# Moving one projection row tile into the attention loop, with early normalisation of half of x and spread stack transfers

## The chip, the core and the metric

The kernel runs on one core of a Trainium2 chip. The metric is the device time of one execution in microseconds (us); three runs of the kernel before gave 1792.6, 1792.7 and 1793.6.

## What is computed

x is 2048 x 640 (S x D). Branch A is self-attention with 32 heads of 20 columns, branch B a two-layer network over the token axis (F = 1728), and a sigmoid gate per token mixes them:

```python
    g = _sigmoid((x * gate_w).sum(-1, keepdims=True))
    a = _A_ref(x, A_wqkv, A_wo)      # softmax(q k^T / sqrt(20)) v, then @ wo
    b = _B_ref(x, B_w1, B_b1, B_w2, B_b2)
    # _B_ref: h = layernorm(x); u = gelu(h^T w1 + b1); y = (u w2 + b2)^T
    return g * a + (1 - g) * b
```

Everything is float32. Products that need it are made of a high and a low float32r part in three passes (high x high, high x low, low x high).

## The kernel before

The kernel is one long stream for TensorE (PE), whose order is written out by hand; ScalarE (ACT), VectorE (DVE), GpSimd (POOL) and SyncE (SP, which issues most transfers) also run in the order in which the code names their instructions. A queue that waits holds up all that is named after it on that queue. Five stages follow each other:

**Projections of q, k and v.** Units of one 128 x 512 output tile (`qk_unit`), 15 matmuls each. ACT copies the high part out of PSUM (`evh`, 3 buffers), DVE subtracts the low part (`evl`, 2 buffers), SP stores both in DRAM. The PSUM tiles go round four banks (`one_tile`). The last 24 units (the loop over `units`, line 545) also prepare the first half of the layer norm for branch B: `h_load` (SP) brings 128 x 320 of x, `h_norm` normalises it on POOL, `h_split` makes the high part on ACT and the low one on POOL. In each unit these stand ahead of the unit's own copies.

**Branch B** (`mlp`). The width D is done in two halves d = 0, 1; each has 14 row tiles of u and 16 of y, in matmuls over 64 rows that go in pairs (`pair64`). Between them the planner (line 796) puts steps of the s stream, which computes raw scores to find the softmax's maxima: `s_one`, `s_over` and `s_two` each use a PSUM bank that DVE's reduction must empty. `dve_room` says how many s steps may have been made at which point. For d = 1 the halves of x are loaded and normalised during d = 0's y tiles, by DVE (`h_norm(1, t)`, line 753). The operand stacks of the next head pair come by many small transfers that are queued in `drip` and issued by SP one per two s steps, among the loads of branch B's weights (`w_raw`, line 512), which ACT and POOL must split before PE uses them. The last stack, for the first attention pair, comes this way too, with the maxima (`load_m`) and `load_v(0)` behind it.

**The attention loop** (line 1005). 16 head pairs x 32 iterations. An iteration issues the score matmuls `st_pair` and `st_one` twice, two s steps while any are left (`take`), and the pv matmuls of the iteration before (`pv_flush`). ACT's three exponentials empty the score banks; the bank pair `two` is there once. The s steps run out in the last pair's iteration 7. After every 16 iterations `pv_evac` copies the result, stores it in `o_d` and the row sums in `l_d`, and `norm_steps` later makes reciprocals and broadcasts them to `r_d`. For the last four heads that chain runs behind the loop (`last_norm`).

**Output projection** (`a_tile`, line 1085). Sixteen row tiles t of 128 rows. Heads 0 to 25 fill four 128-row chunks (`e_load`, `e_high`, `e_low`: load o and the reciprocals, multiply, split), the last heads the fifth (`l_load`, `l_high`, `l_low`). Tiles 0 to 7 use the first four chunks (24 matmuls); from t = 8 each tile uses all five (30), with the missing fifth of tile t - 8 behind it (6). Each tile takes two banks from `st_tile`, which alternates the bank pair `two` and the banks `one0`, `one1`; DVE empties them (line 1072) into `tys`.

## Time and profile before

| | us |
|---|---|
| median of three runs | 1792.7 |
| profiled execution | 1796.8 |
| its span, first to last instruction | 1794.7 |
| PE busy | 1779.3 |
| ACT busy | 1481.1 |
| DVE busy | 1236.7 |
| POOL busy | 640.7 |

The span is one profiled execution; the device time of the same execution is 2.1 us longer, and the median of the runs without a profile is 4.1 us below it. A busy PE counts matmuls from issue to modelled end, so that its share says little where PE waits for less than a matmul's length. TensorE's granted clock is at its full level, 2.4 GHz, in every slice of the page.

### The profile page before, as it was taken

To read this page: it belongs to the slowest core of one execution; us is meant where nothing else is said; L and a number is where in the kernel's file an instruction comes from. 1 tells how busy PE (TensorE), PEld (TensorE's weight loads), DVE (VectorE), ACT (ScalarE), POOL (GpSimd) and SP (SyncE) were. 2 spreads that over 40 slices of the span, in tenths; PEclk is the share of its full clock that TensorE was granted. 3 is DMA by queue.
4 is the path that set the end of the run, shared out by engine and by line. 5 is a ranking of instruction groups with operands and counts; after the bars stand their busy time and mean duration, and the time that the engine had idled before them with its cause. 6 is when DMAs were issued, how large, how long until landed. Compare 5 with 4: busy or idle time off the path is not lost.

```text
span 1794.7 us, 39876 instructions
## 1 busy us (share of the span) xinstructions
PE 1779.3 (99%) x14976; PEld 1113.8 (62%) x14976; DVE 1236.7 (69%) x2394; ACT 1481.1 (83%) x2534; POOL 640.7 (36%) x898
## 2 busy tenths in 40 slices
PE   9999999999999999999999999999999999999998
PEld 7998899999999999633333333333333333333388
DVE  5303289999889999777767677676777777767244
ACT  4244388887878886699999999999999999999930
POOL 1123377778877767211111111121332121212210
PEclk9999999999999999999999999999999999999999
DMA  8757876647675564325213223052363232301653
GB/s 292 241 173 245 258 188 170 161 152 193 175 180 161 144 183 142 90 57 131 59 30 82 61 68 83 18 105 70 46 138 69 52 86 59 73 13 25 216 154 125
DMA packets 157937, 222.95 MB, mean 124 GB/s; under 512 B 68590, under 2 KB 95614, under 8 KB 154318
## 3 DMA queue, kind: packets, MB, share of 16 engines
q1 hardware_dynamic: 139568, 190.74, 39.0%
q0 software_dynamic: 15440, 24.45, 5.8%
q10 hardware_dynamic: 2736, 5.21, 1.0%
q8 instruction: 118, 1.93, 0.5%
q14 instruction: 75, 0.61, 0.1%
HBM read 165.43 MB, written 54.54 MB: 123 GB/s over the span
## 4 chain that ended last, share of the span: by engine, by line
PE 93%; DVE 3%; DMA 3%; ACT 0%; issue 0%; SPq 0%; POOL 0%; ACTq 0%; DVEq 0%; POOLq 0%
PE pv L899 29%; PE st L986 20%; PE s L208 12%; PE u L48 10%; PE y L48 8%; PE qk L54 6%; PE v L54 4%; PE a L1066 3%; DVE mx L214 1%; DMA xr<-in_xT_dram 1%; DVE ov L233 1%; DVE oy L1072 1%; DVE xm L481 1%; DMA wr<-in_w_dram 0%; DMA rbl<-r_d 0%
## 5 line engine op out<-in xcount | busy, mean ns | idle before, releaser
L214 DVE TENSOR_REDUCE mx<-s 128x1 f32<-128x512 f32 x1280 | 834.4, 686 | 282.0 <-PE s L208 216.8
L1001 ACT ACTIVATE p<-st 128x512 f32<-128x512 f32 x1022 | 583.1, 657 | 1.1 <-PE st L986 1.1
L993 ACT ACTIVATE p<-st 128x1024 f32<-128x1024 f32 x511 | 552.4, 1081 | 2.8 <-PE st L986 2.2
L899 PE MATMUL pv<-p,v 128*32 128x512 f32 x4088 | 547.2, 605 | 0.0
L986 PEld LDWEIGHTS st<-qs_True,ks_True 62*128 62x128 f32 x2044 | 245.8, 184 | 432.1 <-ACT p L993 427.0
L986 PE MATMUL st<-qs_True,ks_True 62*128 62x512 f32 x2044 | 495.2, 446 | 0.0
L208 PE MATMUL s<-ks_False,qs_False 60*128 60x512 f32 x1152 | 340.1, 396 | 4.8 <-DVE mx L233 1.9
L43 POOL TENSOR_TENSOR wl<-wr,wh 128x512 fp32r<-128x512 f32 x228 | 275.5, 1219 | 80.3 <-ACT wh L40 64.8
L233 DVE CUSTOM_DVE_ANT_0 ov<-s,ov 128x512 f32<-128x512 f32 x384 | 263.6, 687 | 38.9 <-PE s L208 28.7
L223 ACT ACTIVATE ov<-s 128x512 f32<-128x512 f32 x384 | 226.4, 597 | 68.4 <-PE s L208 62.7
L208 PE MATMUL s<-sk,sq 60*128 60x512 f32 x896 | 279.7, 394 | 0.0
L879 POOL DMA_DIRECT2D l_d<-oev x128 | 62.7, 496 | 459.1 <-DVE oev L872 459.0
L48 PE MATMUL y<-gh,wh 64*128 64x320 f32 x896 | 223.1, 307 | 0.0
L48 PE MATMUL y<-gl,wh 64*128 64x320 f32 x832 | 214.7, 306 | 0.0
L48 PE MATMUL y<-gh,wl 64*128 64x320 f32 x832 | 214.1, 305 | 0.0
L208 PEld LDWEIGHTS s<-ks_False,qs_False 60*128 60x128 f32 x1152 | 190.0, 185 | 11.6 <-DVE mx L233 4.9
L899 PEld LDWEIGHTS pv<-p,v 128*32 128x32 f32 x4088 | 82.6, 108 | 174.9 <-issue 162.4
L40 ACT ACTIVATE wh<-wr 128x512 fp32r<-128x512 f32 (+3 forms) x247 | 147.0, 599 | 43.1 <-PE y L48 15.7
L48 PE MATMUL u<-hh,wh 64*128 64x320 f32 x864 | 178.7, 307 | 0.0
L48 PE MATMUL u<-hl,wh 64*128 64x320 f32 x864 | 178.6, 307 | 0.0
L208 PEld LDWEIGHTS s<-sk,sq 60*128 60x128 f32 x896 | 166.0, 185 | 18.1
L48 PE MATMUL u<-hh,wl 64*128 64x320 f32 x800 | 167.8, 307 | 0.0
(137 smaller groups left out, 2339.3 us busy)
## 6 DMA issues: line engine op xcount, KB each, us to landing
wr<-in_w_dram SPq DMA_DIRECT2D x192, 256.0 KB
ks_True<-k_d SPq DMA_DIRECT2D x96, 160.0 KB
qs_True<-q_d SPq DMA_DIRECT2D x192, 80.0 KB
qs_False<-q_d SPq DMA_DIRECT2D x108, 80.0 KB
sk<-k_d SPq DMA_DIRECT2D x42, 160.0 KB
sq<-q_d SPq DMA_DIRECT2D x84, 80.0 KB
v_d<-vt SPq DMA_DIRECT2D x32, 168.0 KB
v<-v_d SPq DMA_DIRECT2D x16, 336.0 KB
```

Of the source, the lines that this page charges most:

```text
L40: nc.scalar.activation(hi, src, AF.Copy)
L43: (lo_eng or nc.vector).tensor_sub(lo, src, hi.bitcast(F32))
L48: nc.tensor.matmul(ps[k], a[r], b[r], start=start, stop=stop)
L54: nc.tensor.matmul(ps, a, b, start=(i == 0 and k == 0), stop=(i == n - 1 and k == 2))
L208: nc.tensor.matmul(ps, qs[half][r, t * P:(t + 1) * P], ks[r, kc * 512:(kc + 1) * 512], start=True, stop=True)
L214: nc.vector.tensor_reduce(mx[:, slot, j, t: t + 1], ps, axis=AX.X, op=OP.max)
L223: nc.scalar.activation(over[j, kc], ps, AF.Relu)
L233: nc.vector.tensor_tensor_reduce(ov, ps, ov, 1.0, -3.0e38, OP.add, OP.max, mx[:, slot, j, t: t + 1])
L899: nc.tensor.matmul(pv[r: r + 32, :], v_tiles[p][:, kt, 10 * j: 10 * j + 32], pt[j, c], start=(kt == 0), stop=(kt == NT - 1))
L986: nc.tensor.matmul(ps, ks[r, kt * P:(kt + 1) * P], qs[qh][r, c * 512:(c + 1) * 512], start=True, stop=True)
L993: nc.scalar.activation(pt, ps, AF.Exp, scale=SCALE)
L1001: nc.scalar.activation(pt, ps, AF.Exp, scale=SCALE)
```

## The change

Four edits.

- **A projection tile in the loop.** Row tile 0's first four chunks are multiplied inside the last head pair: 24 `pair64` in two halves of 320 columns (`row_half`, `first_row`), one or two per iteration from 10 to 31, in the two `s` banks. `e_load(0)` moves to iteration 0, `e_high(0)` and `e_low(0)` to 5, the second ones to 24. The first iteration of the loop takes no s steps.
- **The last reciprocals.** The last `l_d` stores, their load, the store of the reciprocals (now 4 x 2048 in `rc_d`) and four loads that broadcast them go through SP; o's last chunk is one load. `l_high` goes behind the tile's evacuation.
- **Early normalisation.** In the 24 units x's second half is loaded (`n_load`), normalised by DVE and stored in `xn_d` (`n_store`), both transfers from POOL, in 3 buffers; branch B's second half then loads it ready, and `h_norm(1, t)` goes, with its part of `dve_room`.
- **Spread transfers.** `drip` is issued every fourth s step (every second one before step 128), the first attention stack in the gaps between (`slow`), `load_v(0)` in 8 pieces.

```diff
+    rc_d = dram.tile([LAST, S], F32, name="rc_d")
+    xn_d = dram.tile([S, HALF], F32, name="xn_d")
...
-        nc.sync.dma_start(xm, x[t * P:(t + 1) * P, d * HALF:(d + 1) * HALF])
+        rows = slice(t * P, (t + 1) * P)
+        nc.sync.dma_start(xm, xn_d[rows] if d else x[rows, :HALF])
...
+    def n_load(t):
+        xns[t] = hp.tile([P, HALF], F32, tag="ty", bufs=3, name=f"xn1_{t}")
+        nc.gpsimd.dma_start(xns[t], x[t * P:(t + 1) * P, HALF:])
+
+    def n_store(t):
+        xn = xns.pop(t)
+        nc.vector.tensor_scalar(xn, xn, negm[:, t:t + 1], rstd[:, t:t + 1], op0=OP.add, op1=OP.mult)
+        nc.gpsimd.dma_start(xn_d[t * P:(t + 1) * P], xn)
...
         if 2 <= n < NT + 2:
-            h_norm(0, n - 2)
+            h_norm(n - 2)
+        if 4 <= n < NT + 4:
+            n_store(n - 4)
+        if 2 <= n < NT + 2:
+            n_load(n - 2)
...
-                        h_norm(1, 0)
-                    if t + 1 < NT:
-                        later_on(2500, lambda t=t: h_norm(1, t + 1))
...
     def dve_room(n):
-        norms = min(max((n - U_STEPS) / (NT * 40), 0), 1) * NT * NORM
-        return (dve_work(S_AHEAD) + NT * NORM) * (n + 1 - FIRST) / (STEPS - 20 - FIRST) - norms
+        return dve_work(S_AHEAD) * (n + 1 - FIRST) / (STEPS - 20 - FIRST)
...
             if done == 4 * 128 + 40:
+                held, drip[:] = list(drip), []
                 st_src[0] = base_stack(0, True, None)
...
-                drip.append(lambda: load_v(0))
-            if drip:
+                load_v(0, 8, put)
+                slow[:], drip[:] = drip, held
+            if drip and (done % 4 == 0 or done < 128):
                 drip.pop(0)()
+            elif slow and done % 4 == 2:
+                slow.pop(0)()
...
+    def last_load():
+        b = LAST * S // P
+        rl = ap.tile([P, 256], F32, tag="rl", bufs=1, name="rl_last")
+        nc.sync.dma_start(rl[:, :b], l_d[H - LAST:].rearrange("h (a b) -> (h a) b", b=b))
+        last_rl.append(rl[:, :b])
+
+    def last_recip():
+        nc.vector.reciprocal(last_rl[0], last_rl[0])
+        nc.sync.dma_start(rc_d.rearrange("h (a b) -> (h a) b", b=LAST * S // P), last_rl[0])
...
-                nc.gpsimd.dma_start(l_d[h: h + 1, cols], ev[r + DH: r + DH + 1, :])
+                put = nc.sync if (p, qh) == (NP - 1, 1) else nc.gpsimd
+                put.dma_start(l_d[h: h + 1, cols], ev[r + DH: r + DH + 1, :])
...
+    def l_load():
+        raw, rb = [ap.tile([P, 4, 512], F32, name=f"{n}l") for n in ("or", "rb")]
+        r0 = (NC - 1) * P
+        nc.gpsimd.dma_start(raw.rearrange("p a b -> p (a b)"), o_d[r0:])
+        rb = rb.rearrange("p a b -> p (a b)")
+        nc.gpsimd.dma_start(rb[:L0], r_v[r0:r0 + L0])
...
+    def l_rest(rb):
+        for h in range(LAST):
+            nc.sync.dma_start(rb[L0 + h * DH:L0 + (h + 1) * DH], rc_d[h:h + 1].broadcast_to([DH, S]))
...
+    def row_half(c):
+        row_ps[:] = [s_tile([P, HALF], f"a0_{c}_{k}") for k in range(2)]
+        oh, ol = o_hl[0]
+        cols = slice(c * HALF, (c + 1) * HALF)
+        passes = [e for k in range(NC - 1) for e in ((oh[:, k, :P], woh[k]), (oh[:, k, :P], wol[k]), (ol[:, k, :P], woh[k]))]
+        for i, (a, b) in enumerate(passes):
+            row_mms.append((list(row_ps), a, b[:, cols], i == 0, i == len(passes) - 1))
+
+        def evac(ps=list(row_ps)):
+            for k in range(2):
+                nc.vector.scalar_tensor_tensor(tys[0][:, cols], ps[k], g_t[:, :1], tys[0][:, cols], op0=OP.mult, op1=OP.add)
+
+        row_evacs.append(evac)
+
+    def first_row(it):
+        if it in (10, 21):
+            row_half(it // 21)
+        for _ in range(2 if it in (14, 18, 26) else 1):
+            if row_mms:
+                pair64(*row_mms.pop(0))
+        if it == 19:
+            row_evacs.pop(0)()
...
-                if it in (16, 20, 26, 30):
-                    e_load((16, 20, 26, 30).index(it))
+                if it in (0, 16, 26, 30):
+                    e_load((0, 16, 26, 30).index(it))
...
-                if it in (20, 26):
-                    e_high(it // 26, ap, nc.gpsimd)
-                    e_low(it // 26, nc.gpsimd)
+                if it in (5, 24):
+                    e_high(it // 24, ap, nc.gpsimd)
+                    e_low(it // 24, nc.gpsimd)
...
-            take = min(LEFT - given, 2)
+            take = min(LEFT - given, 2) if p or it else 0
             g = p * 32 + it
             if g:
                 st_pair(g)
+                if p == NP - 1:
+                    first_row(it)
                 st_one(g, 0)
...
     pv_flush()
+    assert not row_mms
+    row_evacs.pop(0)()
...
-        for n in lates:
-            l_high(n)
-        evacs = [(t, range(NC) if t >= NT // 2 else range(NC - 1))]
+        evacs = [(t, range(NC) if t >= NT // 2 else range(NC - 1))] if t else []
...
+        for n in lates:
+            l_high(n)
...
-        if t == 1:
-            last_norm[1][0]()
-            for f in last_norm[2]:
-                f(nc.sync.dma_start)
-            for n in (2, 0, 3, 1):
-                nc.gpsimd.dma_start(*late_args[n][1])
+        if t == 2:
+            last_recip()
+            l_rest(last_rb)
```

## Rows read from the trace of the kernel before

**Rows 1.** The page: busy time, share of the span, instructions

```profile
PE 1779.3 (99%) x14976; PEld 1113.8 (62%) x14976; DVE 1236.7 (69%) x2394; ACT 1481.1 (83%) x2534; POOL 640.7 (36%) x898
```

**Rows 2.** Windows: length, busy PE PEld DVE ACT POOL, clock, DMA share, GB/s

```profile
136.00:220.00 84.00, 84.00 (x362) 67.77 (x361) 24.69 (x38) 31.50 (x58) 28.84 (x35) 1.00 0.80 248
600.00:700.00 100.00, 100.00 (x1235) 99.75 (x1234) 90.71 (x229) 82.90 (x162) 72.51 (x76) 1.00 0.56 161
1668.00:1712.00 44.00, 44.00 (x282) 15.73 (x285) 4.03 (x4) 44.00 (x71) 12.91 (x16) 1.00 0.65 220
```

**Rows 3.** Waits of PE, whole span: us in total, times, longest us

```profile
PE a L1066 <- DVE oy L1072: 3.5, 8, 1.7
PE s L208 <- DVE mx L233: 1.9, 9, 0.3
PE s L208 <- DVE mx L214: 1.3, 1, 1.3
PE s L208 <- ACT ov L223: 1.3, 2, 1.0
```

**Rows 4.** Chain that ended last, branch B: start us, us, what

```profile
393.52 1.02 DVE xm L481
...
459.79 1.02 DVE xm L481
...
521.68 4.72 DMA wr<-in_w_dram
```

**Rows 5.** Timeline of SP's queue, 500 to 528: start us, us, instructions

```profile
514.68 2.08 SPq L808 DMA_DIRECT2D qs_True<-m_d  x3
```

**Rows 6.** Timeline, all engines, first two iterations of the loop

```profile
740.01 0.61 DVE L692 TENSOR_SCALAR ty<-y,omg,b2o 128x320 f32<-128x320 f32 x1 [3.79 <-PE s L208]
...
741.94 1.09 PE L208 MATMUL s<-ks_False,qs_False 60*128 60x512 f32 x2 [1.33 <-DVE mx L214]
...
742.97 1.07 PE L899 MATMUL pv<-pf,v 128*32 128x512 f32 x8
...
743.97 0.50 PE L986 MATMUL st<-qs_True,ks_True 62*128 62x512 f32 x2
```

**Rows 7.** Timeline, all engines, one iteration of the last pair without s steps

```profile
1671.18 0.93 PE L986 MATMUL st<-qs_True,ks_True 62*128 62x512 f32 x4
...
1672.04 0.20 PEld L899 LDWEIGHTS pv<-p,v 128*32 128x32 f32 x8 [0.24 <-issue]
...
1673.08 0.61 PEld L986 LDWEIGHTS st<-qs_True,ks_True 62*128 62x128 f32 x4 [0.84 <-ACT p L993]
```

**Rows 8.** Chain that ended last, from 1705: start us, us, what

```profile
1714.88 7.10 PE a L1066 x47
...
1735.47 7.62 DMA rbl<-r_d
...
1744.94 4.65 PE a L1066 x30
...
1750.68 4.68 PE a L1066 x30
```

**Rows 9.** Timeline of PE, start of projection tile 10

```profile
1756.44 0.56 PE L1066 MATMUL a<-woh,ohe 128*128 128x320 f32 x2 [0.22 <-DVE oy L1072]
1756.84 0.46 PE L1066 MATMUL a<-wol,ohe 128*128 128x320 f32 x2
1757.13 0.46 PE L1066 MATMUL a<-woh,ole 128*128 128x320 f32 x2
```

**Rows 10.** Timeline of DVE, the 24 units: the nineteenth unit's low part

```profile
209.82 0.69 DVE L43 TENSOR_TENSOR evl<-qk,evh 128x512 fp32r<-128x512 f32 x1 [4.79 <-ACT evh L40]
```

**Rows 11.** DMA issues: queue, count, KB each, median us to landing

```profile
xn<-in_x_dram POOLq DMA_DIRECT2D x16, 320.0 KB, 4.1
...
kd_d<-evl POOLq DMA_DIRECT2D x4, 256.0 KB, 5.8
```

**Rows 12.** Groups by shape: count, busy us, mean ns, idle before

```profile
L950 DVE TENSOR_TENSOR ore<-ore,rbe 128x1024 f32<-128x1024 f32 x8 | 10.5, 1308 | 3.6 <-DMA rbe<-r_d 3.6
```

More of the change, by code (lines that the diff above doesn't have):

```diff
@@ L21 @@
 NDIFF = 8
+LAST = 4
 DROWS = 3 * 128
@@ L115, in gated_mix @@
     b2o = cp.tile([P, NT], F32, name="b2o")
-    drip = []
+    drip, slow = [], []
     def load_stack(p, ks, qs, full, eng=nc.sync):
@@ L156, in gated_mix, with load_v @@
     s_src, st_src, v_tiles = {}, {}, {}
-    def load_v(p):
+    def load_v(p, pieces=1, put=nc.sync.dma_start):
         v_tiles[p] = base.tile([P, NT, NPAIR], F32, tag="v", bufs=2, name=f"v{p}")
         c0 = NPAIR * (p % 8)
-        nc.sync.dma_start(v_tiles[p], v_d[p // 8, :, :, c0: c0 + NPAIR].rearrange("t p c -> p t c"))
+        for i in range(pieces):
+            kt = slice(i * NT // pieces, (i + 1) * NT // pieces)
+            put(v_tiles[p][:, kt], v_d[p // 8, kt, :, c0: c0 + NPAIR].rearrange("t p c -> p t c"))
     s_close = []
@@ L475, in h_load, with h_norm @@
         xm = hp.tile([P, HALF], F32, tag="xm", bufs=4, name=f"xm{d}_{t}")
-        nc.sync.dma_start(xm, x[t * P:(t + 1) * P, d * HALF:(d + 1) * HALF])
+        rows = slice(t * P, (t + 1) * P)
+        nc.sync.dma_start(xm, xn_d[rows] if d else x[rows, :HALF])
         xms[d, t] = xm
-    def h_norm(d, t):
-        xm = xms[d, t]
-        (nc.vector if d else nc.gpsimd).tensor_scalar(xm, xm, negm[:, t:t + 1], rstd[:, t:t + 1], op0=OP.add, op1=OP.mult)
+    def h_norm(t):
+        xm = xms[0, t]
+        nc.gpsimd.tensor_scalar(xm, xm, negm[:, t:t + 1], rstd[:, t:t + 1], op0=OP.add, op1=OP.mult)
+    xns = {}
+    def n_load(t):
[5 more added lines that the diff above has]
+        nc.gpsimd.dma_start(xn_d[t * P:(t + 1) * P], xn)
     def h_split(d, t):
@@ L770, in gated_mix @@
     FIRST = 14
-    U_STEPS = (FT - 1) * 48 + 32
-    DIFF, RAW, NORM = 435, 640, 600
+    DIFF, RAW = 435, 640
     def dve_work(k):
@@ L853, in recip, with store @@
             nc.vector.reciprocal(rl[:, i: i + 64], rl[:, i: i + 64])
-        def store(h, put=nc.gpsimd.dma_start):
+        def store(h):
             src = rl[a * (h - h0): a * (h - h0 + 1), :b]
-            put(r_d[h].rearrange("d (a b) -> a d b", b=b), src.unsqueeze(1).broadcast_to([a, DH, b]))
-        return ([load], [lambda i=i: recip(i) for i in range(0, b, 64)], [lambda *a, h=h: store(h, *a) for h in range(h0, h1)])
+            nc.gpsimd.dma_start(r_d[h].rearrange("d (a b) -> a d b", b=b), src.unsqueeze(1).broadcast_to([a, DH, b]))
+        return ([load], [lambda i=i: recip(i) for i in range(0, b, 64)], [lambda h=h: store(h) for h in range(h0, h1)])
+    last_rl = []
+    def last_load():
[6 more added lines that the diff above has]
+        nc.sync.dma_start(rc_d.rearrange("h (a b) -> (h a) b", b=LAST * S // P), last_rl[0])
     later = {}
-    last_norm = []
     def norm(h0, h1, at):
@@ L918, in o_tiles, with o_load @@
         return [pool.tile([P, k, n], dt, tag=name + tag, bufs=bufs, name=f"{name}{tag}{q}") for name in names]
-    def o_load(q, rows, k, n, tag, bufs, eng):
+    def o_load(q, rows, k, n, tag, bufs):
         raw, rb = o_tiles(q, k, n, tag, bufs, ("or", "rb"), ap, F32)
@@ L923, in o_load @@
         o_raw[q, tag] = raw, rb
-        args = [(dst, src.rearrange("(c p) s -> p c s", p=P)[:, :, cols])
-                for dst, src in ((raw, o_d[rows]), (rb, r_v[rows]))]
-        if eng:
-            for a in args:
-                eng.dma_start(*a)
-        return args
+        for dst, src in ((raw, o_d[rows]), (rb, r_v[rows])):
+            nc.sync.dma_start(dst, src.rearrange("(c p) s -> p c s", p=P)[:, :, cols])
     tys = {}
@@ L967, in e_low @@
         o_low(q, "e", o_hl[q], eng)
-    def l_load(q):
-        return o_load(q, slice((NC - 1) * P, D), 1, 512, "l", 4, None)
+    L0 = (H - LAST) * DH - (NC - 1) * P
+    def l_load():
[4 more added lines that the diff above has]
+        nc.gpsimd.dma_start(rb[:L0], r_v[r0:r0 + L0])
+        for q in range(4):
+            o_raw[q, "l"] = raw[:, q:q + 1], rb[:, q * 512:(q + 1) * 512].unsqueeze(1)
+        return rb
+    def l_rest(rb):
+        for h in range(LAST):
+            nc.sync.dma_start(rb[L0 + h * DH:L0 + (h + 1) * DH], rc_d[h:h + 1].broadcast_to([DH, S]))
     def l_high(q):
@@ L1079, in a_tile @@
         return evac
-    late_args = {n: l_load(n) for n in (2, 0, 3, 1)}
-    for n in (2, 0, 3, 1):
-        nc.gpsimd.dma_start(*late_args[n][0])
+    last_rb = l_load()
     e_high(2, lp)
@@ L1105, in gated_mix @@
             l_low(n)
-        if t == 1:
-            last_norm[1][0]()
-            for f in last_norm[2]:
-                f(nc.sync.dma_start)
-            for n in (2, 0, 3, 1):
-                nc.gpsimd.dma_start(*late_args[n][1])
+        if t == 2:
+            last_recip()
+            l_rest(last_rb)
     ordered.close()
```

9 lines of the change are left out of this document (5 added, 4 removed).

## Prediction

> **What bounds the kernel now.** I read the page's busy times first: PE 1779 of 1795 us [rows 1]. What can be won is therefore PE work taken off the path and the few places where PE waits. The windows by stage come next. In the stretch 600 to 700 PE has no idle time at all; the 24 projection units take 84.0 us for 24 units, 3.5 each, without a gap, with the DMA engines 0.80 busy; at the end of the attention loop ACT is busy 44.00 of 44 us and DVE 4 [rows 2]. So branch B and the units are paced by PE, and the end of the loop by ACT. The waits of PE name what is lost: 3.5 us in the output projection behind DVE's evacuations, 1.9 and 1.3 behind DVE's reductions of the s steps, 1.3 behind ACT [rows 3]. The chain and timelines then say which places these are.
>
> **The tile in the loop.** In the last pair, from iteration 8 on, an iteration lasts 1.90 us (1671.18 to 1673.08). PE is through its score matmuls and then waits: its queue sits 0.24 ahead of pv at 1672.04, and the next pair of scores starts only when ACT has left the bank pair [rows 7]. PE needs of the 1.90 about 0.86 - 0.24 ahead of pv and 1.0 for pv, so that 0.25 to 0.3 is free. A `pair64` of 320 columns costs what a 128-row matmul of as many columns costs, since its two halves run side by side; two such matmuls start 0.29 apart [rows 9], so one is 0.147. One per iteration fits; in three iterations there are two, 0.29, about the free time. They stand behind `st_pair` and ahead of pv, where PE waits for ACT anyway: I cost them at nothing, and if that cover is gone at 24 x 0.147 = 3.5 us. DVE is idle there [rows 2], so the two evacuations are free. Behind the loop 24 matmuls go: **-3.5**.
>
> Making o's first chunk at iteration 5 puts a multiplication of 1.3 us [rows 12] among the s steps, while two reductions of DVE fill all but about 0.6 of an iteration. DVE falls 0.7 behind, the two banks cover part: **+0.3** (0 to 0.7). POOL's split of that chunk has five iterations, 9.5 us, until PE needs it in iteration 10.
>
> **The last reciprocals.** Tile 0 starts at 1714.88; eight tiles at 24 x 0.147 = 3.52 bring PE to 1743.0, but tile 8 starts at 1744.94 [rows 8]: 1.9 us lost, as the load of the broadcast reciprocals took 7.62 from 1735.47 and landed at 1743.1, with DVE's evacuations queued behind its multiplication. After the change PE enters tile 8 at 1714.9 + 7 x 3.52 = 1739.5 and needs the fifth chunk 3.5 later, 1743.0. DVE needs some 3.3 for it (five operations of 0.7 to 1.3), so the reciprocals must have landed by 1739.7. They are made behind tile 2's evacuation, near 1725; the store and the load then cost between two landings of an SP or POOL transfer, about 2 x 4 [rows 11], and 2 x 7.6 [rows 8]: 1733 to 1740. The queues moved past: `l_d`'s four stores and the load on SP stand ahead of `e_load(4)`, which is needed only by tile 8; POOL's stores of o come earlier by as much. DVE waits for the row sums with tile 3's evacuation behind it, some 3 us after they have landed. So the stall goes: **-1.9** (0 to -1.9).
>
> Without tile 0 the banks alternate the other way: from tile 8 on the large tile takes `one0` and `one1` in place of the pair. Tiles 8 and 9 start 5.74 apart [rows 8], 36 matmuls are 5.28: 0.46 lost per tile, 0.22 of it shown as a wait for DVE [rows 9], since the pair is free only when both halves are. With separate banks the first matmul can go when the first half is out, the second waits as before: one matmul won per tile, 7 x 0.147, **-1.0** (0 to -3.2).
>
> **No s steps in the first iteration.** DVE is still at branch B's last tile from 740.01 on, and takes the s steps behind it [rows 6]. The two s matmuls of iteration 0 fill both banks, those of iteration 1 wait for DVE 1.33, and pv follows at 742.97, the next scores at 743.97 [rows 6]. Without them iteration 1 finds free banks; its last score tile needs the bank that DVE leaves at 740.6, so it runs until 740.9, pv until 741.9: the next scores start 2.0 earlier. The s steps end one iteration later, in iterations that ACT paces anyway: **-2.0** (-1.0 to -2.0).
>
> **Branch B.** DVE's 16 normalisations stand on the chain, 1.02 us each, nine of them 8.3 us apart [rows 4], and PE's nine waits for `mx` L233, 1.9 us, are theirs; where they don't run, PE waits for nothing [rows 2]. `dve_room` without them spreads the s steps evenly (by its own constants 477 us of DVE work over 2558 steps, 187 ns per step, where it was 175 and 190), so nothing comes in their place: **-1.9** (-1 to -1.9). The two waits for ACT's copies, 1.3 us [rows 3], lie at 510 to 528, where loads of weights land late (4.72 from 521.68 [rows 4]) because the first attention stack's last transfers stand between them on SP, such as three of the maxima's in 2.08 us [rows 5]. At half the rate they get out of the way: **-1.2** (-0.5 to -1.3). A stack of 21 transfers now takes 84 of the 128 s steps that it has, and the first attention stack is through at step 696 of 1074; neither is late.
>
> Sum of the gains: -3.5 + 0.3 - 1.9 - 1.0 - 2.0 - 1.9 - 1.2 = **-11.2**, with the bounds -7 to -13.
>
> **The price: 32 transfers of 160 KB in the 24 units.** This stage carries 20.8 MB in 84 us at a DMA share of 0.80 [rows 2], so 67.2 us of full DMA. The new 5.2 MB at the same rate are 16.9 us: together 84.1, a full stage. Worse, POOL's order becomes a chain. Per unit it is: low part, `h_norm`, store of x(n-4), load of x(n-2). The load reuses the buffer whose store POOL issued one unit before, so a unit can't be shorter than that store's landing less one issue, L - 0.5. Queued behind it on POOL is the layer norm of the first half; behind that, on ACT, the high part of x, and behind that the copy that empties PE's bank. PE tolerates some: a bank is needed again three units, 10.5 us, after its matmuls, of which two copies take 1.4, so 9.1 can be lost. In the kernel before, the nineteenth unit (matmuls done at 136 + 19 x 3.5 = 202.5) already was copied only by 210.5, delayed by ACT's order [rows 10]: 8.0 of 10.5.
>
> L isn't shown. The nearest rows are POOL's loads of 320 KB, 4.1, and its stores of 256 KB, 5.8 [rows 11], both under less DMA traffic or of more bytes. L = 4.1 gives a unit of 3.6, 16 x 0.1 = 1.6 behind, nothing lost; L = 5.8 gives 5.3, 16 x 1.8 - 9.1 = 20 us. I take 4.85, between the ends since neither is nearer: 4.35 a unit, 16 x 0.85 - 9.1 = **+4.5**.
>
> The Trainium skill, page "DMA: Bandwidth & Descriptors", section "Anatomy of one DMA — SWDGE (gpsimd) path", fits such a transfer as 2.0 us plus the bytes over 436 GB/s, an estimate of 2.4 us here. The trace disagrees: its rows of the same queue show 4.1 and more [rows 11]. By the page POOL's chain would be 1.9 a unit and cost nothing, and the time that of the second rival.
>
> **Time.** -11.2 + 4.5 = -6.7. The profiled execution took 1796.8 (span 1794.7 and 2.1 around it) and would take 1790.1; the median of the runs is 4.1 below it, so the forecast is 1792.7 - 6.7 = **1786.0**.
>
> **Rivals.** (1) Slower: the units are held up by POOL's chain and the full DMA engines. It decides above L = 5.5: 16 x (5.0 - 3.5) - 9.1 = 14.9 eats the gains and 0.2% more; at 5.8 the time is 1792.7 - 11.2 + 20 = 1801. For it: DMA work of 84.1 us for 84.0, and the 8.0 us of delay that are there already; against it: 160 KB is less than either row. (2) The units hide it all: 1792.7 - 11.2 = 1781.5, to 1780 with the gains' bounds. For it: PE has no gap there now [rows 2]. (3) The tile isn't hidden, since the loop's cycle from ACT's exponential to the next scores has no room: 1786.0 + 3.5 = 1789.5. Against it: PE's wait of 0.24 and more per iteration [rows 7]. (4) The edit doesn't shorten the reciprocals' way, the 1.9 stays: 1788; part of the forecast's range.
>
> **Chances.** Measurement tells about 0.2% of this kernel, 3.6 us, from no change. Forecast with a loss in the units of 1 to 7.6 us: 0.40; (2) 0.22; (3) 0.08, about half within 0.2%; a loss of 7.6 to 14.8, within 0.2%: 0.18; (1) 0.12. Faster 0.66, same 0.22, slower 0.12. The range 1780 to 1795 leaves out (1) and the ends of the gains.
>
> **What would show it.** Right: no DVE normalisation and no PE wait in branch B; tile 8 some 24.6 us after tile 1; 24 `pair64` in the last pair at an unchanged 1.90 per iteration; iteration 2 of the loop 2 us closer to branch B's end. The units' length against 84.0 shows the price; POOL's waits for the landing of `xn_d`'s stores show its mechanism. The forecast is wrong if the units exceed 84 by more than 8 us or not at all, or if the last pair's iterations grow.

## The result

Twenty runs of each kernel side by side give 1794.8 us for the kernel before (1792.6 to 1798.1) and **1797.7 us for the changed one** (1792.0 to 1801.7): a ratio of 1.0015, with a 95% interval of 1.0009 to 1.0022. The change costs some 3 us where a gain of 6.7 was forecast; the range, 1780 to 1795, misses it. About 2 of the 11.7 us between 1786.0 and 1797.7 are the base: the three runs that the forecast started from lie at 1792.7, the twenty at 1794.8.

The profiled execution took 1792.0 us (span 1790.2) and is the fastest of the twenty. So stages are compared over several profiles. The table has the stages of all kernels, in us, from the start times in PE's timeline. The units go from their first qk matmul to the first u matmul, branch B ("B") from there to the first pv matmul of the loop, the loop from there to the first matmul of a whole projection tile, the projection to the end of the span. A ratio is the time of a kernel over that of the kernel before on the same chip, with its 95% interval; kernels that ran once have their one time.

| kernel | start | units | B | loop | projection | ratio (95%) or one time |
|---|---|---|---|---|---|---|
| before | 135.83 | 84.09 | 523.05 | 971.84 | 79.89 | 1 |
| before again (e16) | 135.69 | 84.09 | 520.19 | 971.86 | 79.07 | 1793.0 |
| after | 135.04 | 90.45 | 516.05 | 971.98 | 76.68 | 1.0015 (1.0009-1.0022) |
| e1 | 138.94 | 84.09 | 518.09 | 971.96 | 79.52 | 0.9981 (0.9970-0.9992) |
| e2 | 135.72 | 91.46 | 520.82 | 973.09 | 77.91 | 1.0053 (1.0036-1.0070) |
| e3 | 136.25 | 88.77 | 518.17 | 971.86 | 80.25 | 1.0006 (0.9994-1.0017) |
| e4 | 134.84 | 84.09 | 513.70 | 971.87 | 78.40 | 0.9964 (0.9951-0.9978) |
| e5 | 137.99 | 89.37 | 520.00 | 972.23 | 80.11 | 1.0004 (0.9994-1.0015) |
| e6 | 134.68 | 91.32 | 517.64 | 971.88 | 76.08 | 1.0009 (1.0000-1.0018) |
| e7 | 136.35 | 89.05 | 515.77 | 972.16 | 77.07 | 1.0000 (0.9990-1.0010) |
| e8 | 135.23 | 84.08 | 519.90 | 972.00 | 75.09 | 1788.4 |
| e9 | 135.84 | 84.09 | 519.32 | 971.84 | 78.21 | 1791.2 |
| e10 | 138.47 | 84.08 | 518.03 | 972.06 | 75.16 | 0.9975 (0.9965-0.9985) |
| e11 | 136.38 | 88.01 | 531.62 | 972.17 | 76.92 | 1.0083 (1.0070-1.0096) |
| e12 | 136.87 | 84.09 | 519.03 | 971.96 | 77.45 | 0.9984 (0.9974-0.9993) |
| e13 | 138.65 | 86.10 | 516.29 | 972.17 | 79.49 | 0.9989 (0.9979-0.9999) |
| e14 | 134.82 | 85.06 | 518.02 | 972.06 | 76.44 | 0.9968 (0.9956-0.9981) |
| e15 | 139.12 | 88.53 | 519.43 | 972.01 | 76.31 | 0.9973 (0.9963-0.9983) |
| e17 | 134.74 | 85.69 | 518.08 | 971.98 | 76.61 | 0.9971 (0.9961-0.9981) |
| e18 | 136.36 | 84.09 | 520.79 | 972.03 | 76.73 | 0.9971 (0.9960-0.9982) |

The start differs by 4 us between executions of the same code, so it says nothing of a change. Stages with the same code repeat within 0.1 us in undisturbed units and within 0.4 in the loop (e2's is 1.2 longer), but only within 3 in B and within 4 in the new projection.

### The profile page after: what moved, and what is told of

Same layout as the page of the kernel before. It is cut to its first block, busy times and chain, and to the rows that moved or that the text cites. A ratio compares the mean times of both kernels' runs of the same rounds, so it can differ in the third digit from the quotient of the medians.

```text
span 1790.2 us, 40007 instructions
## 1 busy us (share of the span) xinstructions
PE 1774.9 (99%) x15000; PEld 1110.4 (62%) x15000; DVE 1237.1 (69%) x2396; ACT 1481.7 (83%) x2534; POOL 649.8 (36%) x919
## 4 chain that ended last, share of the span: by engine, by line
PE 92%; DMA 5%; DVE 2%; issue 1%; ACT 1%; SPq 0%; POOL 0%; DVEq 0%; ACTq 0%
PE pv L930 29%; PE st L1026 21%; PE s L213 13%; PE y L49 10%; PE u L49 10%; PE v L55 4%; PE qk L55 3%; PE a L1135 2%; DMA xr<-in_xT_dram 1%; DMA wr<-in_wqk_dram 1%; DMA xm<-in_x_dram 1%; DMA rc_d<-rl_last 1%; DMA wr<-in_w_dram 0%; DMA rbl<-rc_d 0%; DMA kd_d<-kf 0%
## 5 line engine op out<-in xcount | busy, mean ns | idle before, releaser
L213 PE MATMUL s<-ks_False,qs_False 60*128 60x512 f32 x1152 | 363.2, 394 | 1.5 <-ACT ov L228 1.3
L213 PEld LDWEIGHTS s<-ks_False,qs_False 60*128 60x128 f32 x1152 | 198.6, 185 | 4.7 <-ACT ov L228 2.4
L49 PE MATMUL u<-hh,wh 64*128 64x320 f32 x864 | 201.0, 307 | 0.0
L49 PE MATMUL u<-hl,wh 64*128 64x320 f32 x864 | 200.7, 307 | 0.0
L49 PE MATMUL u<-hh,wl 64*128 64x320 f32 x800 | 189.1, 307 | 0.0
```

Source lines behind the costliest of these rows:

```text
L49: nc.tensor.matmul(ps[k], a[r], b[r], start=start, stop=stop)
L213: nc.tensor.matmul(ps, qs[half][r, t * P:(t + 1) * P], ks[r, kc * 512:(kc + 1) * 512], start=True, stop=True)
```

## The profile after

The windows of the units (length, busy PE PEld DVE ACT POOL, granted clock, DMA share, GB/s), which answer to the first line of [rows 2]:

```profile
164.00:178.00 14.00, 14.00 (x62) 11.34 (x61) 7.24 (x11) 3.98 (x8) 6.58 (x11) 1.00 1.01 345
...
206.00:210.00 4.00, 0.74 (x2) 0.60 (x3) 2.84 (x3) 0.47 (x1) 3.22 (x6) 0.68 0.92 268
210.00:214.00 4.00, 4.00 (x11) 3.15 (x10) 1.13 (x2) 1.58 (x4) 2.06 (x3) 0.50 1.03 354
```

Where the kernel before had a DMA share of 0.80 and no gap, the share is now about 1 for stretches, PE does almost nothing from 206 to 210, and the four microseconds behind that run at a granted clock of 0.50, 1.2 GHz in place of 2.4: 11 matmuls in 4 us, where the first line has 62 in 14. Of the 6.4 us that the units grew, the wait is 3.8 and this stretch 2.3, as PE's timeline shows (in brackets the idle time before, and what ended it): eleven matmuls in 4.83 us from 209.26 on, where eleven at the full clock take 2.5, at one per 0.23:

```profile
205.06 0.40 PE L55 MATMUL qk<-xh,wl 128*128 128x512 f32 x1
209.26 0.77 PE L55 MATMUL qk<-xh,wh 128*128 128x512 f32 x1 [3.81 <-DVE evl L44]
...
214.09 0.47 PE L55 MATMUL qk<-xh,wl 128*128 128x512 f32 x1
```

The waits of 136 to 226 (engine and line, what was waited for: us in total, times, longest):

```profile
POOL xm L487 <- DMA xm<-in_x_dram: 25.2, 8, 13.5
ACT hh L41 <- POOL xm L487: 24.5, 11, 5.8
DVE xn L497 <- DMA xn<-in_x_dram: 23.6, 9, 5.3
...
POOL xn L493 <- DMA xn_d<-xn: 9.1, 5, 4.6
```

The last line is the chain that the prediction priced. The others are two that it did not: DVE's early normalisation waits for its loads with the units' low parts queued behind it, and POOL waits for the loads of x's first half.

In the projection, the chain that ended last (start, us, what) shows the reciprocals' way, to be read beside [rows 8]:

```profile
1724.32 9.37 DMA rc_d<-rl_last
...
1734.80 5.92 DMA rbl<-rc_d
...
1740.90 1.30 DVE orl L977 x2
```

and the timelines of POOL, DVE and PE show what stood in its way and what it cost:

```profile
1719.51 0.56 POOL L1001 DMA_DIRECT2D orl<-o_d  x1 [2.89 <-DMA o_d<-oev]
```

```profile
1730.79 1.23 DVE L977 TENSOR_TENSOR ore<-ore,rbe 128x1024 f32<-128x1024 f32 x1 [5.40 <-DMA rbe<-r_d]
```

```profile
1732.62 0.78 PE L1135 MATMUL a<-woh,ohe 128*128 128x320 f32 x2 [1.25 <-DVE oy L1141]
...
1745.60 0.53 PE L1135 MATMUL a<-woh,ohl 128*128 128x320 f32 x2 [1.05 <-DVE oy L1141]
...
1747.11 0.87 PE L1135 MATMUL a<-woh,ohe 128*128 128x320 f32 x2 [0.39 <-DVE oy L1141]
```

POOL's 1.4 MB for o's last chunk now go out in two transfers from 1719.5 on, among SP's chunk loads of 1 MB each. The 32 KB of reciprocals, stored at 1724.3 behind all of these, took 9.4 us, and the broadcasts landed at 1740.7, 16.4 us after the store was issued; a chunk load issued at 1719.3 held DVE until 1730.8. From 1758.7 on PE has no gap, where before it lost 0.22 to 0.32 at each tile [rows 9].

## Experiments

### The early normalisation, taken away and alone (e1, e2)

e1 is the changed kernel with this edit undone, e2 the kernel before with this edit alone:

```diff
-        if 4 <= n < NT + 4:
-            n_store(n - 4)
-        if 2 <= n < NT + 2:
-            n_load(n - 2)
...
+                        h_norm(1, 0)
+                    if t + 1 < NT:
+                        later_on(2500, lambda t=t: h_norm(1, t + 1))
```

> The changed kernel without the early normalisation alone (the 16 loads, normalisations and stores of the units are gone, DVE normalises in branch B again). Theory A (the 24 units pay for everything that is lost): the units are back at 84.0 us with no PE wait, the gains of the other three edits stay: 7.0 - 1.9 of branch B and the loop's start, 3.2 of the projection, so about 8 below the kernel before, 1786 to 1788 beside 1794.8. Theory B (the runs of the changed kernel lose their time elsewhere, in the loop or the projection): within 2 us of the changed kernel, 1796 to 1799.

> The kernel before with the early normalisation alone. Theory A: the units grow from 84.0 to 90 us or more, with a PE wait of some 4 us and a stretch at the lower clock behind it, branch B gains 1.9: slower than before by 4 to 10 us, 1799 to 1805. Theory B: units and time within 2 us of the kernel before.

Both say theory A in sign. Undone, the units are back at 84.09 and the ratio falls from 1.0015 to 0.9981, 6 us; alone, it costs 0.53%, 9.5 us. But e1's median of 1791.6 is 3.6 us above the upper end of what theory A has, and its table row names the place: the projection takes 79.5 us, not 76.7. Its PE timeline there, and two windows:

```profile
1742.86 0.56 PE L1123 MATMUL a<-woh,ohl 128*128 128x320 f32 x2 [1.36 <-ACT ohl L967]
1744.53 0.56 PE L1123 MATMUL a<-woh,oll 128*128 128x320 f32 x2 [0.83 <-DVE oll L973]
1746.15 0.87 PE L1123 MATMUL a<-woh,ohl 128*128 128x320 f32 x2 [1.05 <-DVE oy L1129]
...
1752.28 0.48 PE L1123 MATMUL a<-woh,ole 128*128 128x320 f32 x2
```

```profile
1744.00:1748.00 4.00, 2.41 (x9) 2.13 (x9) 4.00 (x7) 0.75 (x1) 0.00 (x0) 0.69 0.77 257
1748.00:1752.00 4.00, 4.00 (x16) 3.89 (x15) 2.20 (x4) 0.31 (x1) 0.00 (x0) 0.50 0.44 169
```

Three waits at tile 8 add to 3.2 us, and behind them the granted clock falls to 0.50: the eleven pairs of matmuls from 1746.15 to 1752.28 take 6.13 us, where eleven pairs at the full clock take 3.2 (0.29 each), so 2.9 us more. The profile of the changed kernel escaped that second half, and so did e6; e3, e5 and e13 have it as e1 does, e4, e7 and e12 in a shorter form (one window of 4 us at 0.58 to 0.63).

### What in it costs (e4, e3, e5, e13)

e4 keeps every instruction and moves 4 KB in place of 160, and so leaves out the normalisation of branch B's second half; e3 gives the loads six buffers; e5 also takes them two units later; e13 also issues the loads of x's first half one unit earlier.

```diff
# e4
-        nc.gpsimd.dma_start(xns[t], x[t * P:(t + 1) * P, HALF:])
+        nc.gpsimd.dma_start(xns[t][:, :8], x[t * P:(t + 1) * P, HALF:HALF + 8])
...
# e3, e5, e13
-        xns[t] = hp.tile([P, HALF], F32, tag="ty", bufs=3, name=f"xn1_{t}")
+        if t % 2:
+            xns[t] = hp.tile([P, 512], F32, tag="over", bufs=3, name=f"xn1_{t}")[:, :HALF]
+        else:
+            xns[t] = hp.tile([P, HALF], F32, tag="ty", bufs=3, name=f"xn1_{t}")
# e5, e13
-        if 4 <= n < NT + 4:
-            n_store(n - 4)
+        if 6 <= n < NT + 6:
+            n_store(n - 6)
# e13
-        if 1 <= n < NT + 1:
-            h_load(0, n - 1)
+        if n < NT:
+            h_load(0, n)
```

> The changed kernel with 8 of 320 columns in the early loads, normalisations and stores (4 KB in place of 160 KB each); branch B's second half then reads x not normalised, so that part of the result is left out. Order, instructions and three buffers stay. Theory A2 (bytes): units at 84 us, time about 1785. Theory A1: the same if the landing of the small store is under 4.0 us (a 40 KB store took 2.4 us in the projection of the changed kernel); units above 86 us would say that the instructions and their order cost the time, not the bytes.

> The changed kernel with six buffers for the early normalisation in place of three; all transfers and their order stay. Theory A1 (POOL waits for the landing of a store that it issued one unit before, and layer norm, split and PSUM copies stand behind): the load now reuses a buffer whose store is four units old, the waits of POOL for xn_d's stores (9.1 us before) go, the units take 84 to 86 us, and the time is 1785 to 1789. Theory A2 (the DMA engines are full, and the transfers of the units themselves are late): the units stay at 90 us or more and the time at 1796 to 1799.

> The changed kernel with six buffers and the early normalisation two units later (x of unit n-6 in place of n-4), so that DVE takes a load that was issued four units before, not two; all transfers stay. Theory A3 (DVE waits 22 us for these loads even with six buffers, with the copies of the units and with them SP's stores and loads behind it): the units take 84 to 86 us, branch B starts without a wait, 1785 to 1789 us. Theory A2 (the DMA engines are full): units at 88 us or more as with six buffers alone, 1794 to 1797 us.

> The changed kernel with six buffers and the later normalisation (as in the run with the late store) and, beside that, the loads of x's first half one unit earlier on SP. All transfers and bytes stay. Theory E (a closed circle in the order of the queues: SP's loads of x stand behind its stores of the unit before, POOL's normalisation waits 33 to 36 us for them, ACT's split and the copies of the unit behind it, the stores behind these): with a unit more of room the units take 84 to 86 us and branch B starts without a wait: 1785 to 1789 us. Theory A2 (the DMA engines themselves are full): units 88 us or more, 1794 to 1797 us.

With small transfers the units are at 84.09: neither the 48 instructions nor their order cost anything by themselves. That alone doesn't tell bytes from POOL's chain, since the small stores land in 3.9 us, at which the prediction's chain would cost nothing either. e3 tells: six buffers take POOL's wait for its own stores away, and the units only come down from 90.5-91.5 (after, e6, e2) to 88.8; DVE's wait taken away too (e5), they stay at 89.4. So A1 and A3 both miss, and the mechanism that the prediction priced is worth about 2 of 7 us. The waits that are left in e5 are these:

```profile
POOL xm L487 <- DMA xm<-in_x_dram: 36.0, 12, 12.2
DVE evl L44 <- ACT evh L41: 27.0, 10, 5.2
```

SP issues x's loads behind the stores of the unit before, so a late copy makes a late store, a late load, a late split on ACT and a late copy again. One unit of room there (e13) takes POOL's wait for x from 36.0 to 7.0 us and brings the units to 86.1 with all bytes still moved. The same code takes 85.1 in e14 and 88.5 in e15, and 85.7 in e17, where loads and stores run two units earlier. So theory E is worth 2.6 of the 5.1 us that are left (86.6 in the mean of e13 to e15 against 89.2 of e5 and e7), and one profile of three hardly has it; the ratios say 0.9989 against e5's 1.0004, with intervals that just overlap. In e13 the wait moves on to DVE, whose two buffers of `evl` wait for their stores to land:

```profile
DVE evl L44 <- DMA q_d<-evl: 18.3, 6, 5.5
...
POOL xm L487 <- DMA xm<-in_x_dram: 7.0, 5, 2.2
```

No run gives `evl` more buffers, so it stays open whether that wait or the full DMA engines make the rest. e17 has a DMA share near 1 for 48 us in which PE has no gap. Branch B then starts with a wait for ACT, which itself waited 2.4 us for a store of the units to land; a lower clock (0.57 in a window of 4 us) follows.

```profile
160.00:184.00 24.00, 24.00 (x105) 19.43 (x104) 10.86 (x17) 7.10 (x15) 16.38 (x26) 1.00 0.99 335
184.00:208.00 24.00, 24.00 (x104) 19.44 (x103) 8.56 (x14) 7.34 (x14) 13.98 (x22) 1.00 0.97 324
```

```profile
227.42 0.50 PE L211 MATMUL s<-ks_False,qs_False 60*128 60x512 f32 x1 [2.51 <-ACT ov L226]
```

### The projection (e12, e6, e7, e14, e15)

e12 is e1 with the reciprocals behind tile 1. e6 is the changed kernel with that, and with POOL's 1.4 MB on SP behind them; e7 is e6 and e5 together.

```diff
# e12, e6, e7
-        if t == 2:
+        if t == 1:
             last_recip()
             l_rest(last_rb)
# e6, e7
-        nc.gpsimd.dma_start(raw.rearrange("p a b -> p (a b)"), o_d[r0:])
...
+        if t == 2:
+            l_most(last_raw, last_rb)
```

> The changed kernel without the early normalisation, and the last reciprocals made behind tile 1 in place of tile 2; all else as changed. Theory C (the store stood behind the second chunk load of 1 MB on SP, which DVE's place behind tile 2 let pass): the store is issued 2.5 us earlier and ahead of that load, lands in 4 to 7 us in place of 8 to 9.4, the broadcasts land before tile 8's fifth chunk needs them, the projection takes 73.5 to 76 us in place of 79.5, the time is 1786.5 to 1789 us. Rival (POOL's 1.4 MB, issued before it, hold it up all the same): projection 77 to 80 us, 1789 to 1792 us.

> The changed kernel with another order in the projection: reciprocals one tile earlier (behind tile 1), and the 1.4 MB of o's last chunk, which POOL issues at the projection's start, on SP behind them. Theory C (the store of the reciprocals took 9.4 us since it queued behind these 1.4 MB and the loads of the chunks): the reciprocals land before tile 8, no wait over 0.5 us at tiles 6, 8 and 9, no stretch at the lower clock, the projection takes 73 to 74.5 us in place of 76.7 to 80.3, the time is 1791 to 1794 us. Theory D (store and load are slow by themselves): the projection stays at 76.7 us or more, 1796 to 1799 us.

> The changed kernel with both edits, six buffers with the later normalisation and the other order in the projection. Theories A3 and C: units 84 to 86, branch B to the first pv 514, loop 971.9, projection 73 to 74.5, so 1779 to 1783 us. Theories A2 and C: 1788 to 1791 us. Theories A2 and D: 1794 us or more.

Theory C is right on the store and wrong on the time. In e6 the store, no longer behind the 1.4 MB, landed 3.6 us after its issue, when SP issued the broadcasts that wait for it (3.8 in e7):

```profile
1722.26 0.34 SPq L892 DMA_DIRECT2D rc_d<-rl_last  x1
1725.88 1.42 SPq L1012 DMA_DIRECT2D rbl<-rc_d  x4
```

But the 1.4 MB themselves then came last and DVE took o's last chunk only at 1742.4. In e12 the store still took 8.6 us, the broadcasts were in time, and the chunk load behind them was late. SP's queue and DVE's timeline in e12:

```profile
1718.68 0.34 SPq L880 DMA_DIRECT2D rc_d<-rl_last  x1
1727.31 1.42 SPq L998 DMA_DIRECT2D rbl<-rc_d  x4
```

```profile
1737.74 1.23 DVE L965 TENSOR_TENSOR ore<-ore,rbe 128x1024 f32<-128x1024 f32 x1 [6.88 <-DMA rbe<-r_d]
```

Each order moves the wait to another transfer (PE lost 2.7 at one place in e12, 2.2 at three in e6), since some 5 MB must come in between 1717 and 1742 (three chunks of 1 MB, the 1.4 MB and the broadcasts). In the profiles they gain 1.6 to 3.0 us on the changed kernel's 79.1 (mean of after, e1, e3, e4, e5, e13); in the ratios e6 gains 1 us on the changed kernel and e12 nothing on e1. e7 misses its 1779 to 1783 on both counts.

e14 is e13 with the way of the reciprocals as before the change; e15 is e14 with them behind tile 2:

```diff
-        if t == 1:
+        if t == 2:
             last_norm[1][0]()
```

> The kernel of the run before this one with the way of the last reciprocals as it was before the change. Theory F (the new way costs the projection 1.5 to 5 us): the projection takes 75 to 76.5 us, where the new way took 76.7 to 80.3. With theory E in the units: 1781 to 1785 us; with theory A2: 1789 to 1793 us.

> The same with the reciprocals behind tile 2 in place of tile 1, stores and loads as before the change. It tells what the place alone does. Behind tile 1 DVE waited 4.4 us for the row sums, and PE lost 2.0 at tile 4; behind tile 2 this wait goes (gain up to 2.0), while the broadcasts land 2 to 3 us later, near the time when tile 8 needs them. If the place makes the projection of the changed kernel slow: 77 us or more. If the path through 1 MB loads does: 73.5 to 75.5 us.

The old way takes 76.4, in five profiles (e8, e10, e14, e17, e18) 75.1 to 76.7, mean 76.0: **3 us less than the new one, in the profiles**. The ratios say 0.9968 against 0.9989 (e13), and 0.9975 and 0.9971 (e10, e18) against 0.9981 (e1), so 1 to 4 us, with intervals that overlap. What tells the five apart is the clock: behind a wait of about 2 us at tile 4, e8 and e10 keep the full clock, and e14, e17 and e18 have a window of 4 us at 0.57 to 0.62. The same window of e10 and of e14, from the matmuls behind that wait:

```profile
1726.00:1730.00 4.00, 4.00 (x27) 4.00 (x28) 3.79 (x6) 0.57 (x2) 0.21 (x1) 1.00 0.99 212
```

```profile
1723.00:1727.00 4.00, 4.00 (x17) 3.92 (x17) 3.30 (x5) 0.58 (x2) 0.01 (x1) 0.58 0.95 198
```

e15 shows that the place is not it: 76.3 behind tile 2 as well, where a wait of 1.8 at tile 8 stands in for one of 1.9 at tile 4. e14's 1788.9 lies between its two theories. What the new way bundles (the path through `rc_d`, SP's `l_d` stores, o's last chunk in one load, `l_high` behind the evacuation) is told apart only as far as e6 and e12 do it.

### The other parts (e8, e9, e10, e16)

e8 is the kernel before with spread transfers and the tile, e9 with the first iteration and the new reciprocals, e10 with spread transfers, tile and first iteration; e16 is the kernel before again. Their diffs are the change's own hunks; the one line of the first iteration is

```diff
-            take = min(LEFT - given, 2)
+            take = min(LEFT - given, 2) if p or it else 0
```

> The kernel before with the spread transfers and the tile in the loop alone (first iteration, reciprocals and normalisation as before). By the prediction's sizes: branch B to the first pv 523.1 - 1.2 = 521.9 us, the loop unchanged at 971.8, the projection 79.9 - 3.5 for the tile, but the old way of the reciprocals lands at the same time, so the 3.5 comes back as a longer wait at tile 8, and the other alternation of the banks gives 1 to 2: 78 to 79 us. Rival: the spread gives more than its visible waits of 1.3 us, branch B under 520 us.

> The kernel before with the free first iteration and the new way of the reciprocals alone (no tile in the loop, stack transfers and normalisation as before). Theory (the parts add up): branch B to the first pv 523.1 - 1.8 = 521.3 us, since the step from the spread transfers with the tile (519.9) to the same with the free first iteration (518.1) was 1.8. Projection: with tile 0 still behind the loop, the reciprocals have 3.5 us more, so the waits at tiles 8 and 9 are 0 to 2 us; 79 to 81 us in all. Rival (spread and first iteration work on the same waits): branch B 519 to 520 us.

> The kernel before with the spread transfers, the tile in the loop and the free first iteration; the way of the reciprocals and the normalisation stay as before. Theory (the new way of the reciprocals and the early normalisation cost time, the other three parts gain): units 84.1, branch B 518.1, loop 971.9, projection 75 to 76.5 us, 1786 to 1788 us beside 1795 of the kernel before, and 3 to 5 below the changed kernel without the early normalisation. Rival (the projection's 75.1 us of the run with spread and tile was luck of the DMA queues): projection 77 to 80 us, 1789 to 1792 us.

> The kernel before once more, for a second look at how long its stages take: start 136, units 84.1, branch B to the first pv 521 to 523, loop 971.8, projection 78 to 80 us.

e8 beats its expectation, and e10 has the stages of its theory with a median of 1789.9, 2 us above it. In both, once tile 0 was gone, the old way of the reciprocals came earlier by itself. The timelines of DVE and POOL in e8:

```profile
1721.84 0.55 DVE L860 RECIPROCAL rl<-rl 128x64 f32<-128x64 f32 x1 [4.39 <-DMA rl<-l_d]
```

```profile
1728.41 2.12 POOL L1147 DMA_DIRECT2D rbl<-r_d  x4 [8.63 <-DMA r_d<-rl]
```

The loads go out 17.2 us after the projection's start, where it was 20.1 (1734.9 - 1714.8), and DVE multiplies at 1733.7 without a wait, 22.5 after the start, where they landed after 28.3 [rows 8]. No PE wait is left at tile 8, only 2.0 at tile 4, where DVE waits for the row sums. Nor is the wait at tile 8 that the edit was to remove the same in every execution with tile 0 still behind the loop: 1.7 in the first profile of the kernel before, 0.9 in the second (e16), none in e2, whose projection is that of the kernel before. e9 has the new way with tile 0 behind the loop: a wait of 0.8 at tile 9, and a projection of 78.2, where the three with the old way have 77.9 to 79.9; its branch B is the rival's (519 to 520). The second profile of the kernel before takes the ground from under the spread transfers. PE's waits in B, beside [rows 3]:

```profile
PE s L208 <- DVE mx L233: 1.9, 9, 0.3
PE s L208 <- DVE mx L214: 1.3, 1, 1.3
```

The 1.3 us behind ACT that the edit was to remove aren't there, and B is 2.9 us shorter; e18, with the spread, has 1.8 of them again. They come and go from one execution to the next. The 1.3 us behind `mx` L214 (the line has another number in each kernel) is in both profiles, in e8 and in e2, and in none with the free first iteration.

### Half the dose, and the best of it (e11, e17, e18)

e11 is e10 with the early normalisation for 6 of 16 tiles. e17 is e14 with all of it two units earlier, e18 is e10 again beside it.

```diff
# e11
+        if 4 <= n < EARLY + 4:
+            n_store(n - 4)
+        if 2 <= n < EARLY + 2:
+            n_load(n - 2)
...
# e17, against e14
-        if 6 <= n < NT + 6:
-            n_store(n - 6)
-        if 2 <= n < NT + 2:
-            n_load(n - 2)
+        if 4 <= n < NT + 4:
+            n_store(n - 4)
+        if n < NT:
+            n_load(n)
```

> The kernel of the run before this one, with the early normalisation for 6 of the 16 tiles only, in units 2 to 9, where the DMA share before was 0.62 (136 to 160 us). Theory A2 (bytes on top of DMA engines that are nearly full): 1.9 MB in this stretch fit, the units stay at 84.1 us, branch B loses 6 of the 16 normalisations, 1.6 of 4.4 us: 1784.5 to 1787 us. Rival (POOL's chain of loads and stores costs time wherever it stands): the units grow by 1 to 4 us, 1788 to 1791 us.

> The kernel with six buffers, loads of x one unit ahead and the old way of the reciprocals, with the whole early normalisation two units earlier (loads in units 0 to 15, stores in 4 to 19), so that it is over before branch B's first weights are loaded. Theory E with late weights (what is left of the early normalisation's price, a wait of 2.2 to 2.7 us at branch B's start and 1.7 of lower clock behind it, comes from transfers in the last units that delay the weights): the wait goes, units 84.1 to 86, branch B 513.7 to 516, 1784 to 1787 us. Rival (the DMA engines are full over the whole stage, the time of the transfers in it does not matter): units and the wait as before, 1788 to 1791 us.

> The kernel before with spread transfers, the tile in the loop and the free first iteration once more, beside the run before this one on the same chip: stages as in its first run (units 84.1, branch B 518, loop 972, projection 75.2), 1788 to 1790 us. If theory E with late weights holds, the run before this one is 2 to 5 us faster; if its rival does, they are within 1.5 us.

e11 missed: its median of 1808.7 is 18 us above the upper end of its rival. The units grew by 3.9 with 1.9 MB, more than half of what 5.2 MB cost: a share that fits on average doesn't fit in that order of queues. The other 13.6 us are in B: 9.7 more of PE's idle time than in e10 (three waits of 2.6 for DVE, told below, and 3.5 for ACT, of which 2.1 at B's start as in the kernels with all 16 tiles) and 3.9 of busy time, with a lower clock behind two of the waits. The three waits hit normalisations that DVE still does there and that now fall among POOL's work; they are a matter of order and not of the early transfers, though no run shows which line of the edit moved them. e17 and e18 have the same ratio: in its best form here, the early normalisation gives back in the units and at B's start (85.7 + 518.1 = 603.8) what it saves (84.1 + 518.0 and 520.8 = 602.1 and 604.9). Fastest are e10, e14, e15, e17 and e18, by about 0.3%, 5 us, on the kernel before, and e4, by 0.36%, with that part of the work left out; e1, e12 and e13 gain 0.1 to 0.2%.

## Why the prediction was wrong, point by point

By stages, with the means of the profiles: units +6.8 (after, e6), B -4.8 against both profiles of before, loop +0.1, projection -0.4 (79.1 against 79.5), in sum +1.7, where the times say +2.9. The forecast had +4.5, -5.1, +0.3 and -6.4. **The projection is where it failed**, by 6.0 us, then the units, by 2.3; B agrees by errors that cancel, which is luck. The bounds -7 and -13 of its sum of gains are not the sums of the terms' own ends, which are -5.3 and -13.8. Of its signs of being wrong none came true; only tile 8's start, 26.2 us after tile 1's in place of 24.6, pointed at the projection.

- **Tile in the loop, -3.5**: right in the loop, which takes 971.86 to 972.23 with the tile's 24 matmuls (972.0 in the mean) and 971.84 to 971.86 without (973.09 once, in e2), so that the tile and DVE's earlier multiplication cost 0.2 together, not 0.3. What it gives in the projection depends on the reciprocals: with the old way 76.0 against 77.9 to 79.9, with the new one nothing (79.1 against 78.2 in e9's one profile), since PE then comes to tile 8 sooner and waits.
- **The last reciprocals, -1.9: the step that failed**, and in sign. Store and load were to take 8 us, 4 each, or 15.2 at most, and the stall was counted as gone; they took 16.4 (1724.3 to 1740.7). The 4 came from x's loads of 320 KB, issued one per 2.2 us; the store had some 3.4 MB of POOL and SP issued in the 5 us before it and took 9.4 (8.2 to 9.4 in the six profiles of the mean of 79.1), and 3.6 without POOL's 1.4 MB (e6). And the stall that was to be removed goes by itself once the tile is gone (e8), and even with the tile in e2. Instead of -1.9 the new way is +3.1 against the old one in the profiles, 1 to 4 by the ratios; rival 4 allowed only for no gain.
- **Banks, -1.0**: undersized. Tiles start 5.55 apart (1747.11 to 1780.38, six tiles) where it was 5.79 (1750.68 to 1785.41), so 0.24 x 7 = 1.7.
- **First iteration, -2.0**: the named wait of 1.3 goes; e9 gives -0.9 to -3.7 against the two profiles, e18 and e10 against e8 from +0.9 to -1.9. In size it is not settled.
- **Branch B's normalisation, -1.9**: undersized. The nine waits go, but with the early normalisation free of charge (e4) B takes 513.7, where the same code takes 518.0 to 520.8 (e1, e10, e12, e18), so 4.3 or more: 1.9 less idle (against e10), and 2.4 less of PE's busy time with as many matmuls. Delays shorter than a matmul stand in no list of waits. The nine that stand 8.3 apart in the chain are also not DVE's work alone: DVE's instruction takes 1.10 in them and 0.44 at its shortest, and ends each time just behind an instruction of POOL, as told below. Whether another place for them would have won the same is not tried.
- **Spread transfers, -1.2**: not supported. It was read from two waits of one execution.
- **The units, +4.5**: too low, and by another mechanism. The landing L was well estimated: 4.85 taken, 4.6 measured for the stores. By the sum, 4.6 gives 16 x 0.6 - 9.1 = 0.5; measured are 6.4 to 7.4, and 1.3 to 2.8 of waits at B's start. The step that failed is the cover of 9.1: the sentence behind it says that 8.0 of 10.5 were in use. With the 2.5 left the sum is 7.1, near the measured one, but the runs don't bear that out as the cause, since six buffers gain only 2. What was left out is SP's order, worth 2.6 more in the mean; the remaining 2.5 stay open. Rival 1 had the right sign and place, but not the mechanism: L was not above 5.5.
- **The reading of [rows 11]**: that the trace shows 4.1 and more on POOL's queue holds for the rows that were taken. The same queue's 40 KB stores of o took 2.3 us in the kernel before. For the busy stage the higher rows were the right ones: 4.6 and 5.0 were measured there.

## What to carry to other kernels

Price a transfer by what is queued ahead of it where it will stand, not by its median in another stretch; and when a stage has DMA busy 0.8 and engines that wait for each other's transfers, count the delay that is already there before calling the rest cover. Work that stands in the list of waits of a single execution may not be there in the next: a gain of 1 us wants a second profile.

## What the runs showed of the hardware

**Size hardly matters to a landing in a busy stage.** e4's transfers of 4 KB (last column: median us from issue to landing):

```profile
xn<-in_x_dram POOLq DMA_DIRECT2D x16, 4.0 KB, 3.8
xn_d<-xn POOLq DMA_DIRECT2D x16, 4.0 KB, 3.9
```

With 160 KB they took 5.0 and 4.6 in the changed kernel, for 40 times the bytes. The DMA share of the stage was 0.67 to 0.89 in e4 and 0.70 to 0.99 in the changed kernel. The Trainium skill, page "DMA: Bandwidth & Descriptors", section "Anatomy of one DMA — SWDGE (gpsimd) path", would give 2.0 us for 4 KB as an estimate. The trace's 3.8 and 3.9 in this stage are nearly twice that.

**DVE can wait inside an instruction.** In e11 a normalisation of 128x320, 0.44 us when undisturbed, ran 4.12 us three times, from 416.51, 452.52 and 488.87. POOL's timeline and DVE's:

```profile
416.27 0.89 POOL L718 TENSOR_TENSOR ty<-ty,x 128x320 f32<-128x320 f32 x1
417.12 0.87 POOL L44 TENSOR_TENSOR hl<-xm,hh 128x320 fp32r<-128x320 f32 x1
417.95 2.49 POOL L44 TENSOR_TENSOR wl<-wr,wh 128x512 fp32r<-128x512 f32 x2
```

```profile
416.51 4.12 DVE L486 TENSOR_SCALAR xm<-xm,negm,rstd 128x320 f32<-128x320 f32 x1
```

It began while POOL ran and ended 0.2 us after the last of four POOL instructions that follow without a gap (420.44); each time PE lost 2.6, and twice a lower clock followed (0.65 in the window of 4 us from 420). The Trainium skill, page "SBUF — State Buffer", section "Who interferes with whom", says that a DVE instruction of the kind `tensor_scalar`, when it runs in a mode that uses both of DVE's port pairs, and a GpSimd one exclude each other: the first has the shared pair for its whole instruction, and the other blocks. The trace agrees that DVE was held, and goes further: DVE got no turn between POOL's four. That it ran in that mode is not shown. In the kernel before (and in e10), nine of the 16 normalisations take 1.10 in place of 0.44, the nine that stand 8.3 apart in [rows 4]. All nine end 0.18 us behind the POOL instruction that was running when they began; the first of them, from the timelines of POOL and DVE:

```profile
393.06 1.30 POOL L43 TENSOR_TENSOR wl<-wr,wh 128x512 fp32r<-128x512 f32 x1 [2.15 <-ACT wh L40]
```

```profile
393.43 1.10 DVE L481 TENSOR_SCALAR xm<-xm,negm,rstd 128x320 f32<-128x320 f32 x1
```

There POOL also went on without a gap, and DVE still had its turn behind the first instruction; what decides this is not shown. Such a delay is shown as busy time of DVE, and no list of waits has it.

**The granted clock.** A wait of PE can have two prices. Behind the 3.8 us in the units came a stretch at 0.50 that cost 2.3 us more, and behind e1's three waits in the projection, 3.2 us together, one that cost 2.9. The waits of the changed kernel in the projection, 2.7 together, had no such stretch; nor had e8 and e10 behind 2.0 and 2.1 at tile 4, where e14, e17 and e18 had one at 0.57 to 0.62 behind 1.9 to 2.4.
